# Decay attention and max-of-three experts on one core: the attended tokens of a later batch are split column part by column part

## The chip, the core and the metric

The kernel runs on one core of a Trainium2 chip. A core has TensorE (PE: matmuls, with a weight load, PEld, ahead of each), VectorE (DVE), ScalarE (ACT), GpSimd (POOL) and SyncE (SP), which here issues all transfers. The metric is the device time of one execution in microseconds, as the median of several runs. [...]

## What is computed

```python
# q, k, v: (8, 8, 576, 64); f: (8, 8, 576)
scores = scale * np.matmul(q, k.transpose(0, 1, 3, 2))
cum = np.cumsum(np.log(np.clip(f, 0.0001, 1.0)), axis=-1)
scores = np.where(causal, -1000000000.0, scores + cum[:, :, :, None] - cum[:, :, None, :])
attn = softmax(scores)                       # with 1e-09 added to the sum
x = np.matmul(attn, v)                       # to (4608 tokens, 512)
h = np.maximum(np.maximum(x @ w1, x @ w2), x @ w3)   # three experts, 512 -> 768
out = h @ w_out                              # 768 -> 512
```

## The kernel before

There are eight batches of eight heads. A batch has 576 tokens and, after attention, 512 features, held as four tiles u of 128 features by 576 tokens (one tile for two heads). Attention of a head works in two units of its 576 queries: unit 2 is queries 0 to 255, unit 1 is queries 256 to 575. Each has a first pass of matmuls (scores), a maximum over keys (DVE, then a POOL all-reduce), a second pass that subtracts it, exponentials on ACT, and, for two heads at a time, the matmuls with the values (line 771 in batch 0, line 802 later) into the one PSUM bank t (mp 132 for unit 2 of batch 0). The sums of a pair of heads go through a small transfer to memory and back, and line 908 multiplies u by their inverse. In batch 0 the division is done in four groups: lines 846 (turning the sums), 861 and 862 (DVE), 850 (widening on ACT), 857 (spreading on PE), 868 (the multiplication on DVE).

The experts need each value of x as a rounded part xh and a remainder xl, because the matmuls take rounded operands: `split_x` copies u to xh on ACT (line 913) and subtracts on DVE (line 915), once for each of the four tiles of a batch, over all 576 columns. There is one buffer xh and one xl, so the split of a batch overwrites that of the batch ahead.

`moe` runs the experts in two runs of columns. An even batch takes columns 0 to 255 and then 256 to 575; an odd one 0 to 319 and then 320 to 575. A run has 18 first-product tiles (`gemm1`, line 939): 12 matmuls each, three for each of the four tiles of x, into one of three PSUM banks (mp 130, 131, 132, in rotation). ACT (line 946) or DVE (line 948, the running maximum of the three experts) empties the bank; then ACT and DVE split the maximum (lines 951, 953). After each run come the output products (`gemm2`, line 968, 18 matmuls for 128 tokens), also into the three banks.

Nothing is issued in the order in which it is written. `Plan.add` collects every step with its engine, a cost, the keys that it reads and writes, and a priority. `Plan.emit` then plays all engines forward with these costs and picks, for each engine, among the steps that are ready the one of lowest rank: its priority less a share (BLW) of the length of what hangs on it. Each engine runs its steps in the resulting order. A key stands for a buffer or a part of one; `plan.parts` says which keys are made of smaller ones, and a step waits for the last writer and, where it writes, for all readers of each of its parts. The priorities are head numbers with offsets: LEAD, UP, VO (values), FO (finishing a pair), XO (split), HP and VP (transfers of heads and values), QP and QP1 (transfers and transposes of four heads, lines 535 to 541), LO (the groups of batch 0), WP and WR (weights, lines 512 to 522), HC, SP_, CB, MLAG and lag. MORE adds a delay to what another engine has to deliver, and LIKE is how far PE goes out of rank to put like matmuls together.

Of the kernel before, what the change touches and what calls it, by code (L numbers as in the profile page):

```python
# [48 lines left out]
class Plan:  # L49
# [9 lines left out]

    ROOM = {"PE": (0.93, 0), "ACT": (1.0, -20.0), "DVE": (1.0, 0.0), "POOL": (1.0, 400.0), "SP": (1.0, 0)}  # L60
    LATE = 350.0
    MORE = (0.0, 100.0, 125.0, 0.0, 250.0)
    LIKE, HOLD = 4.0, 0.4

    def __init__(self):
        self.steps, self.wrote, self.read, self.parts = [], {}, {}, {}
# [20 lines left out]
    def emit(self):  # L87
# [8 lines left out]
        for i in reversed(range(n)):  # L96
            s = self.steps[i]
            down[i] = s[1] + s[5] + max((down[u] + 150 for u in users[i]), default=0.0)
        BLW = 0.19
        rank = [s[4] * 1.0 - BLW * down[i] / 12000 for i, s in enumerate(self.steps)]  # L100
        free, wait, live = {}, {}, {}
        for i, s in enumerate(self.steps):
# [69 lines left out]
def act_cost(cols):  # L172
    return 0.833 * cols + 60


def dve_cost(cols):
    return 1.04 * cols + 68
# [3 lines left out]
def kernel(  # L181
# [15 lines left out]
    nc = tc.nc  # L197
# [21 lines left out]
    for i in range(8):  # L219
        for c in ("q", "k"):  # L220
            plan.parts[f"{c}f{i}"] = [f"{c}f{i}/{x}" for x in range(4)]
            plan.parts[f"{c}s{i}"] = [f"{c}s{i}/{x}" for x in range(4)]
    for i in range(4):
        plan.parts[f"vn{i}"] = [f"vn{i}/{x}" for x in range(3)]
    plan.parts["r"] = ["r/0", "r/1"]
    plan.parts["sc"] = ["sc/0", "sc/1"]
# [81 lines left out]
    def U(i):  # L308
        return UT[i] if i < KT else lazy(f"u{i}", [P, S], F32)
# [10 lines left out]
    def xh(kt):  # L320
        return lazy("xh", [P, KT, S])[:, kt, :]

    def xl(kt):
        return lazy("xl", [P, KT, S])[:, kt, :]
# [583 lines left out]
        add("DVE", dve_cost(S), lambda: nc.vector.tensor_tensor(U(i), U(i), R(), op=ALU.mult), [f"u{i}", "r"], [f"u{i}"], prio)  # L908

    def split_x(b, prio):  # L910
        for kt in range(KT):
            i = (b * KT + kt) % NU
            add("ACT", act_cost(S) + 50, lambda i=i, kt=kt: nc.scalar.activation(xh(kt), U(i), AF.Copy),
                [f"u{i}"], [f"xh{kt}"], prio)
            add("DVE", dve_cost(S), lambda i=i, kt=kt: nc.vector.tensor_tensor(
                xl(kt), U(i), xh(kt).bitcast(F32), op=ALU.subtract), [f"u{i}", f"xh{kt}"], [f"xl{kt}"], prio)


    mcount = [0]
# [7 lines left out]
    def gemm1(b, c0, cn, fb, parts, prio):  # L927
        ti = tmc[0] % 2
        tmc[0] += 1
        t, kt_ = TM[ti][:, 0:cn], f"tm{ti}"  # L930
        early = b < NB32 and c0 == 0
        for i in range(3):
            mp, km = next_mp()
            m = mp[:, 0:cn]
            for kt in range(KT):
                def go(kt=kt, i=i, m=m):
                    hh, ll = (xa(kt), xb(kt)) if early else (xh(kt)[:, c0:c0 + cn], xl(kt)[:, c0:c0 + cn])
                    for x, (w, xx) in enumerate(((0, hh), (0, ll), (1, hh))):
                        nc.tensor.matmul(  # L939
                            m, unit_w(i, fb)[:, w, kt, :], xx,  # L940
                            start=kt == 0 and x == 0, stop=kt == KT - 1 and x == 2,
                        )
                add("PE", 3 * mm_cost(cn, P), go,
                    ([f"xa{kt}", f"xb{kt}"] if early else [f"xh{kt}", f"xl{kt}"]) + [f"wh{3 * fb + i}", f"wl{3 * fb + i}"] + ([km] if kt else []), [km], prio)
            if i == 0:
                add("ACT", act_cost(cn), lambda m=m: nc.scalar.activation(t, m, AF.Copy), [km], [kt_], prio)  # L946
            else:
                add("DVE", dve_cost(cn), lambda m=m: nc.vector.tensor_tensor(t, m, t, op=ALU.max),  # L948
                    [km, kt_], [kt_], prio)
        for hh, hl, kh, kl, a, d, w in parts:  # L950
            add("ACT", act_cost(w) + 40, lambda hh=hh, a=a, d=d, w=w: nc.scalar.activation(  # L951
                hh()[:, fb, d:d + w], t[:, a:a + w], AF.Copy), [kt_], [kh + str(fb)], prio)
            add("DVE", dve_cost(w), lambda hh=hh, hl=hl, a=a, d=d, w=w: nc.vector.tensor_tensor(  # L953
                hl()[:, fb, d:d + w], t[:, a:a + w], hh()[:, fb, d:d + w].bitcast(F32), op=ALU.subtract),
                [kt_, kh + str(fb)], [kl + str(fb)], prio)
# [47 lines left out]
                done += 18 * mm_cost(512, P)  # L1003


    LEAD, MLAG, WP, WR = 2.1, -0.1, 0.7, 0.55
    DP = -10.9
    DPW = 4.0
    ROWS = -4.0
    warm_up()  # L1010
    decay()
    QP = -0.3
    UO = 1
    LO = -2.55
    UP, VO, FO, XO = 0.4, 1.8, 0.25, -3.1
    HP, VP = -1.8, 0.6
    SP_ = 1.25
    HC, VO1, XO1, QP1, CB = -0.8, -1.0, -2.3, 0.7, -0.15
    order = (1, 2) if UO else (2, 1)
    for n in range(H):  # L1020
        load_raw(n, n - 9.9)
    for n in range(H):
        turn_head(n, n - 5.6)
        if n % 2 == 0:
            load_v(n // 2, n - LEAD - VP)
    for unit, up in ((2, 0.0), (1, 0.7)):
        for n in range(H):
            p = n * 0.5 - LEAD + up
            subs = (2,) if unit == 2 else ("a", "b") if 0 else ("b", "a")
            for x in subs:  # L1030
                scores(n, x, p)
            for x in subs:
                values(n, x, p + VO1)
            if n % 4 == 3:
                finish_group(n // 4, unit, p + LO)
# [15 lines left out]
    retire(["vn1"], [f"hdh{x}" for x in fbs])  # L1051
    for t in ("hmh", "hml"):
        retire([c + t for c in ("mx", "pf")] + [f"mx{t}a"], [f"{t}{x}" for x in fbs])
    lag = 0.15
    moe(0, lambda x: H + lag + H * x)
    retire([f"rs{g}{u}" for g in range(2) for u in (1, 2)], ["ph1"])
    retire([f"xa{x}" for x in range(KT)], ["pl1"])
# [11 lines left out]
    for n in range(H, BH):  # L1069
# [14 lines left out]
        if n % 2:  # L1084
            finish_pair(pi, p + FO)
        if h == H - 1:
            split_x(b, p + XO)
            moe(b, lambda x, n=n: n + 1 + MLAG + H * x)
    with tc.manual_schedule():
        plan.emit()  # L1090
# [30 lines left out]
```

## Time and profile before

| | |
|---|---|
| runs | 908.95, 909.64, 911.47 us (median 909.64) |
| the profiled execution | 907.59 us, of which 905.5 us is the span of its instructions |
| split on ACT (line 913) | 28 instructions, 0.68 us each, the first at 189.7 us, the last at 824.6 |
| split on DVE (line 915) | 28 instructions, median 0.754 us, longest 1.273 |

A row of the page for an engine gives its busy time, its share of the span and its number of instructions. A row of the waits is: engine, tile and line, what it waited for, then the total in us, how often, and the longest. A group by line gives the shape of what is written and read, the count, then busy time in us and the mean of one in ns, then the idle time of the engine just before. A row of a timeline gives start and duration in us, and in brackets the engine's idle time before it with what ended it; the record of a matmul is longer than the step from one matmul to the next, since matmuls overlap.

### The profile page before, as it was taken

The numbers are of one execution on the slowest core, as the hardware profiler recorded it, in microseconds if no ns is written. First come the engines' busy times: TensorE is split into PE (matmuls) and PEld (weight loads), VectorE is DVE, ScalarE is ACT, GpSimd is POOL, SyncE is SP. The second block draws the span as 40 slices with busy tenths as digits, with TensorE's granted clock in tenths as the row PEclk, the third lists the DMA queues.
The fourth block names the chain that finished last, engine by engine and source line by source line (L and its number), as shares of the span: only waits on it lengthen the run. The fifth ranks groups of instructions, "written<-read, shape, count | busy, mean of one in ns | idle before, by whom it ended". The sixth has DMA issues, their size and how long they took to land.

```text
span 905.5 us, 18417 instructions
## 1 busy us (share of the span) xinstructions
PE 894.0 (99%) x6682; PEld 808.5 (89%) x6682; DVE 643.5 (71%) x1451; ACT 387.5 (43%) x900; POOL 426.8 (47%) x380
## 2 busy tenths in 40 slices
PE   8999999999999999999999999999999999999998
PEld 6899988889989898988989898998989898998998
DVE  6899985577859786786858887786957678672211
ACT  6886644354334443443434443444434443342111
POOL 5444233336455645646554765556555564650000
PEclk9999999999999999999999999999999999999999
DMA  7955155555454455446445554546434455401000
GB/s 205 319 153 177 45 155 128 149 127 161 97 149 123 116 137 147 121 93 181 95 107 143 134 136 117 153 92 175 98 98 130 117 158 118 105 15 37 1 35 24
DMA packets 96868, 110.32 MB, mean 122 GB/s; under 512 B 51861, under 2 KB 64405, under 8 KB 96778
## 3 DMA queue, kind: packets, MB, share of 16 engines
q1 hardware_dynamic: 96778, 109.15, 45.7%
q8 instruction: 53, 0.87, 0.4%
q14 instruction: 37, 0.30, 0.1%
HBM read 49.56 MB, written 9.86 MB: 66 GB/s over the span
## 4 chain that ended last, share of the span: by engine, by line
PE 94%; DVE 2%; ACT 2%; DMA 1%; issue 1%; SPq 0%; ACTq 0%; DVEq 0%
PE mp L939 50%; PE mp L968 17%; PE s L646 13%; PE t L802 9%; PE t L771 2%; PE t L821 1%; DMA w<-in_moe_w_dram 1%; PE mp L771 1%; PE s L662 0%; ACT hl L539 0%; PE t L857 0%; SPq L438 0%; ACT ph_f L734 0%; PE mp L646 0%; DVE va_s L750 0%
## 5 line engine op out<-in xcount | busy, mean ns | idle before, releaser
L939 PE MATMUL mp<-xh_r,w_r 128*128 128x320 f32 (+1 forms) x2160 | 462.2, 298 | 1.4 <-DVE tm L948 1.4
L939 PEld LDWEIGHTS mp<-xh_r,w_r 128*128 128x128 f32 x2160 | 355.8, 188 | 10.9 <-issue 6.0
L939 PE MATMUL mp<-xl_r,w_r 128*128 128x320 f32 (+1 forms) x1080 | 319.5, 296 | 0.0
L758 POOL PARTITION_ALL_REDUCE z<-va_s x96 | 193.1, 2012 | 162.3 <-DVE va_s L750 61.2
L716 POOL PARTITION_ALL_REDUCE gm<-mx x131 | 158.4, 1211 | 194.8 <-DVE mx L703 77.5
L939 PEld LDWEIGHTS mp<-xl_r,w_r 128*128 128x128 f32 x1080 | 203.3, 188 | 0.5
L948 DVE TENSOR_TENSOR tm<-mp,tm 128x256 f32<-128x256 f32 (+1 forms) x192 | 86.3, 449 | 88.6 <-PE mp L939 83.5
L646 PEld LDWEIGHTS s<-qs_r,ks_r 128*128 128x128 f32 (+1 forms) x784 | 116.1, 181 | 19.5 <-issue 14.3
L646 PE MATMUL s<-qs_r,ks_r 128*128 128x320 f32 (+4 forms) x784 | 132.5, 285 | 0.2 <-issue 0.2
L968 PE MATMUL mp<-w_r,hmh_r 128*128 128x512 f32 (+1 forms) x396 | 122.8, 392 | 0.0
L706 DVE TENSOR_TENSOR mx<-mx,s 128x320 f32<-128x320 f32 (+3 forms) x248 | 92.2, 372 | 18.7 <-PE s L646 6.0
L968 PEld LDWEIGHTS mp<-w_r,hmh_r 128*128 128x128 f32 x396 | 70.1, 188 | 13.6 <-issue 1.8
L951 ACT ACTIVATE hmh_r<-tm 128x256 fp32r<-128x256 f32 x96 | 39.9, 416 | 98.9 <-DVE tm L948 98.4
L968 PE MATMUL mp<-w_r,hml_r 128*128 128x512 f32 (+1 forms) x198 | 76.9, 388 | 0.0
L946 ACT ACTIVATE tm<-mp 128x256 f32<-128x256 f32 (+1 forms) x96 | 39.6, 412 | 80.4 <-PE mp L939 76.2
L535 DVE STREAM_TRANSPOSE hl<-hl 128x576 f32<-128x576 f32 x56 | 68.1, 1241 | 0.8 <-DMA hl<-in_k_dram 0.8
L734 ACT ACTIVATE pf<-s 128x512 f32<-128x512 f32 (+4 forms) x107 | 48.8, 505 | 37.5 <-PE s L646 34.5
L953 DVE TENSOR_TENSOR hml_r<-tm,hmh_r 128x256 fp32r<-128x256 f32 x96 | 48.5, 506 | 18.1 <-ACT hmh_r L951 17.5
L719 POOL CAST qs_r<-gm 1x256 fp32r<-1x256 f32 (+1 forms) x112 | 56.8, 508 | 7.1
L675 DVE TENSOR_TENSOR s<-s,mask 128x256 f32<-128x256 f32 x96 | 40.6, 423 | 23.6 <-PE s L646 23.2
L734 ACT ACTIVATE ph_f<-s 128x384 f32<-128x384 f32 x80 | 36.0, 505 | 44.6 <-PE s L646 44.5
L713 ACT ACTIVATE mx<-s 128x320 f32<-128x320 f32 x56 | 24.4, 436 | 51.8 <-DVE s L680 44.1
(213 smaller groups left out, 1261.6 us busy)
## 6 DMA issues: line engine op xcount, KB each, us to landing
qs_r<-hl SPq DMA_DIRECT2D x168, 144.0 KB
ks_r<-hl SPq DMA_DIRECT2D x168, 144.0 KB
w<-in_moe_w_dram SPq DMA_DIRECT2D x18, 512.0 KB
out_dram<-o_r SPq DMA_DIRECT2D x35, 256.0 KB
hl<-in_q_dram SPq DMA_DIRECT2D x14, 576.0 KB
hl<-in_k_dram SPq DMA_DIRECT2D x14, 576.0 KB
r_r<-rdram SPq DMA_DIRECT2D x56, 144.0 KB
vn<-in_v_dram SPq DMA_DIRECT2D x30, 128.0 KB
```

Source lines behind the costliest of these rows:

```text
L535: add("DVE", 1085, lambda e=e, tt=tt, xs=xs: nc.vector.transpose(tt[:, e], xs[:, e]), [key + "0"], [key + "1"], prio)
L646: nc.tensor.matmul(bank[bk][0:l.shape[-1], col:col + w], l, rhs(qa, w), start=start and bk not in begun, stop=stop, skip_group_check=True)
L706: nc.vector.tensor_tensor(mt[:, a:a + w], mt[:, a:a + w], bank[bk][:, col:col + w], op=ALU.max)
L716: add("POOL", 450 + 2.6 * nq, lambda: nc.gpsimd.partition_all_reduce(gm, mt, P, bass.bass_isa.ReduceOp.max), [km, km + "a"], [kg], prio - CB)
L719: add("POOL", 130 + 0.9 * nq, lambda: nc.gpsimd.tensor_copy(QS(s)[96:97, 1, q0:q0 + nq], gm[96:97, :]), [kg], [kx], prio - CB)
L734: add("ACT", act_cost(w), lambda bk=bk, w=w, col=col: nc.scalar.activation(px()[:, col:col + w], bank[bk][:, 0:w], AF.Exp, scale=sc), [kb[ ...
L758: add("POOL", 520 + 5.1 * nq, lambda: nc.gpsimd.partition_all_reduce(Z[:, q0:q0 + nq], blocks_sum()[:, q0:q0 + nq], P, bass.bass_isa.Reduc ...
L802: nc.tensor.matmul(t[D * j:D * j + D, qa:qa + w], vn[:, j, c, 0:D], prs[j][0]()[:, col:col + w], start=x == 0, stop=True, skip_group_check ...
L939: nc.tensor.matmul(m, unit_w(i, fb)[:, w, kt, :], xx, start=kt == 0 and x == 0, stop=kt == KT - 1 and x == 2,)
L948: add("DVE", dve_cost(cn), lambda m=m: nc.vector.tensor_tensor(t, m, t, op=ALU.max), [km, kt_], [kt_], prio)
L953: add("DVE", dve_cost(w), lambda hh=hh, hl=hl, a=a, d=d, w=w: nc.vector.tensor_tensor(hl()[:, fb, d:d + w], t[:, a:a + w], hh()[:, fb, d:d ...
L968: nc.tensor.matmul(mp[:, 0:cn], l[:, fb, cs], unit_o(fb)[:, r, ds], start=fb == 0 and x == 0, stop=fb == FT - 1 and x == 2,)
```

## The change

The split of a later batch is made in parts of columns, with a key for each part of xh and xl (0: columns 0 to 255, 1: 256 to 319, 2: 320 to 575). Ahead of an even batch there are two pieces for each tile, columns 0 to 255 and 256 to 575; ahead of an odd batch three, 0 to 255, 256 to 319 and 320 to 575. A first-product step reads only the keys of the columns of its run, so that a piece of the next batch's split waits only for the run that reads its columns. The first piece has its own priority offset (XO), the others XO + X2. Some twenty of the plan's constants change with it.

```diff
-    MORE = (0.0, 100.0, 125.0, 0.0, 250.0)
-    LIKE, HOLD = 4.0, 0.4
+    MORE = (0.0, 100.0, 125.0, 50.0, 250.0)
+    LIKE, HOLD = 3.5, 0.4
...
-        BLW = 0.19
+        BLW = 0.25
...
+        for t in "hl":
+            plan.parts[f"x{t}{i}"] = [f"x{t}{i}/{x}" for x in range(3)]
...
-        for kt in range(KT):
-            i = (b * KT + kt) % NU
-            add("ACT", act_cost(S) + 50, lambda i=i, kt=kt: nc.scalar.activation(xh(kt), U(i), AF.Copy),
-                [f"u{i}"], [f"xh{kt}"], prio)
-            add("DVE", dve_cost(S), lambda i=i, kt=kt: nc.vector.tensor_tensor(
-                xl(kt), U(i), xh(kt).bitcast(F32), op=ALU.subtract), [f"u{i}", f"xh{kt}"], [f"xl{kt}"], prio)
+        for x, c0, cn in ((0, 0, S2), (1, S2, S1)) if b % 2 == 0 else ((0, 0, S2), (1, S2, 64), (2, S1, S2)):
+            ks = ["0"] if x == 0 else ["1", "2"] if cn == S1 else [str(x)]
+            for kt in range(KT):
+                i = (b * KT + kt) % NU
+                cs, ku = slice(c0, c0 + cn), f"u{i}/{1 + (x == 0)}"
+                kh, kl = ([f"x{t}{kt}/{k}" for k in ks] for t in "hl")
+                add("ACT", act_cost(cn) + 50, lambda i=i, kt=kt, cs=cs: nc.scalar.activation(xh(kt)[:, cs], U(i)[:, cs], AF.Copy),
+                    [ku], kh, prio(x))
+                add("DVE", dve_cost(cn), lambda i=i, kt=kt, cs=cs: nc.vector.tensor_tensor(
+                    xl(kt)[:, cs], U(i)[:, cs], xh(kt)[:, cs].bitcast(F32), op=ALU.subtract), [ku] + kh, kl, prio(x))
...
-                    ([f"xa{kt}", f"xb{kt}"] if early else [f"xh{kt}", f"xl{kt}"]) + [f"wh{3 * fb + i}", f"wl{3 * fb + i}"] + ([km] if kt else []), [km], prio)
+                    ([f"xa{kt}", f"xb{kt}"] if early else [f"x{t}{kt}/{k}" for t in "hl" for k in "012" if c0 <= (0, S2, S1)[int(k)] < c0 + cn]) + [f"wh{3 * fb + i}", f"wl{3 * fb + i}"] + ([km] if kt else []), [km], prio)
...
-    LEAD, MLAG, WP, WR = 2.1, -0.1, 0.7, 0.55
-    DP = -10.9
+    LEAD, MLAG, WP, WR = 2.1, -0.1, 0.4, 0.45
+    DP = -11.15
...
-    QP = -0.3
+    QP = -0.5
...
-    LO = -2.55
-    UP, VO, FO, XO = 0.4, 1.8, 0.25, -3.1
-    HP, VP = -1.8, 0.6
-    SP_ = 1.25
-    HC, VO1, XO1, QP1, CB = -0.8, -1.0, -2.3, 0.7, -0.15
+    LO = -3.35
+    UP, VO, FO, XO = 0.4, 1.4, 0.25, -2.6
+    HP, VP = -2.8, 1.6
+    SP_ = 1.75
+    X2 = -0.5
+    HC, VO1, XO1, QP1, CB = 0.6, -1.0, -2.3, -0.3, 0.35
...
-    for unit, up in ((2, 0.0), (1, 0.7)):
+    for unit, up in ((2, 0.0), (1, 1.0)):
...
-    lag = 0.15
+    lag = 0.3
...
-            split_x(b, p + XO)
+            split_x(b, lambda x: p + XO + (0.0 if x == 0 else X2))
```

Three places show how the order of instructions moves. In the changed file the same statements stand two lines lower up to `finish_pair` (L535 is L537, L908 is L910) and seven lines lower in the experts (L948 is L955); the split is L922.

The first place is DVE at the change from batch 0 to batch 1, where three of the four tiles of x are there. Before:

```order
L948 TENSOR_TENSOR tm_123<-mp_131,tm_123 128x320
L953 TENSOR_TENSOR hml_r<-tm_123,hmh_r 128x256
L953 TENSOR_TENSOR hdl_r<-tm_123,hdh_r 128x64
L908 TENSOR_TENSOR u_89<-u_89,r_r 128x576
L915 TENSOR_TENSOR xl_r<-u_r,xh_r 128x576
L675 TENSOR_TENSOR s_128<-s_128,mask 128x2x128
L680 TENSOR_TENSOR s_126<-s_126,mask 128x64
L701 COPY mx_83<-s_128 128x128
```

Now:

```order
L955 TENSOR_TENSOR tm_123<-mp_131,tm_123 128x320
L960 TENSOR_TENSOR hml_r<-tm_123,hmh_r 128x256
L960 TENSOR_TENSOR hdl_r<-tm_123,hdh_r 128x64
L910 TENSOR_TENSOR u_89<-u_89,r_r 128x576
L922 TENSOR_TENSOR xl_r<-u_89,xh_r 128x256
L922 TENSOR_TENSOR xl_r<-u_r,xh_r 128x256
L922 TENSOR_TENSOR xl_r<-u_r,xh_r 128x64
L922 TENSOR_TENSOR xl_r<-u_88,xh_r 128x64
L922 TENSOR_TENSOR xl_r<-u_88,xh_r 128x256
L677 TENSOR_TENSOR s_128<-s_128,mask 128x2x128
L682 TENSOR_TENSOR s_126<-s_126,mask 128x64
L703 COPY mx_83<-s_128 128x128
```

One subtraction of a whole tile ahead of the masks has become five of parts; the first parts of the two other tiles were made some thirty to sixty instructions earlier.

The second place is PE in the second run (256 columns) of batch 1: w6, w7 and w9 are the weights of tiles that follow one another in the program, mp1 and mp2 two of the three banks. Before:

```order
L939 MATMUL mp1_131<-xl_r_1200,w6_r_695 128x256
L939 MATMUL mp1_131<-xh_r_978,w6_r_695 128x256
L939 MATMUL mp2_132<-xh_r_978,w7_r_699 128x256
L939 MATMUL mp2_132<-xl_r_1200,w7_r_699 128x256
L939 MATMUL mp2_132<-xh_r_978,w7_r_699 128x256 x2
```

Now:

```order
L946 MATMUL mp1_131<-xl_r_1171,w6_r_670 128x256
L946 MATMUL mp1_131<-xh_r_982,w6_r_670 128x256
L946 MATMUL mp1_131<-xh_r_982,w9_r_837 128x256
L946 MATMUL mp1_131<-xl_r_1171,w9_r_837 128x256
L946 MATMUL mp1_131<-xh_r_982,w9_r_837 128x256 x2
```

Before, the tile of w7 lies between two tiles of the bank mp1; now the tile of w9 follows that of w6 on the same bank, and w7 comes after it.

The third place is ACT at the second group of batch 0, where u_88 and u_89 from t are the copies that empty the bank t, and the L539 row is the rounding of four heads' transposed keys or queries. Before:

```order
L512 ACTIVATE w_107<-w_107 128x512
L539 ACTIVATE hl<-hl 128x1152
L783 ACTIVATE u_88<-t 64x160
L785 ACTIVATE ph_79<-t 1x160
L850 ACTIVATE rx<-hdl 128x256
```

Now:

```order
L785 ACTIVATE u_89<-t 64x160
L787 ACTIVATE ph_79<-t 1x160
L736 ACTIVATE pf_80<-s_126 128x480
L514 ACTIVATE w_109<-w_109 128x512
L736 ACTIVATE pf_80<-s_127 128x224
L541 ACTIVATE hl<-hl 128x1152
L852 ACTIVATE rx<-hdl 128x256
```

Before, the rounding stands in front of a copy from t; now it stands behind those copies and in front of the widening.

More of the change, by code (lines that the diff above doesn't have):

```diff
@@ L1011 @@
     decay()
-    QP = -0.3
+    QP = -0.5
     UO = 1
-    LO = -2.55
-    UP, VO, FO, XO = 0.4, 1.8, 0.25, -3.1
-    HP, VP = -1.8, 0.6
-    SP_ = 1.25
-    HC, VO1, XO1, QP1, CB = -0.8, -1.0, -2.3, 0.7, -0.15
+    LO = -3.35
[4 more added lines that the diff above has]
+    HC, VO1, XO1, QP1, CB = 0.6, -1.0, -2.3, -0.3, 0.35
     order = (1, 2) if UO else (2, 1)
     for n in range(H):
-        load_raw(n, n - 9.9)
+        load_raw(n, n - 10.1)
     for n in range(H):
```

## The prediction

> **What bounds the kernel now.** I read the page first, its span, its engines and the slices.
>
> ```profile
> span 905.5 us, 18417 instructions
> ...
> PE 894.0 (99%) x6682; PEld 808.5 (89%) x6682; DVE 643.5 (71%) x1451; ACT 387.5 (43%) x900; POOL 426.8 (47%) x380
> ...
> PEclk9999999999999999999999999999999999999999
> ```
>
> TensorE is busy for 894.0 of 905.5 us, and the granted clock never drops. No other engine is near its limit. So the change can win only part of 905.5 - 894.0 = 11.5 us, unless it changes the matmuls themselves. The next view cuts the span into seven stretches, to see where the 11.5 us lie.
>
> ```profile
> core 0: us, PE busy (x) PEld busy (x) DVE busy (x) ACT busy (x) POOL busy (x), PEclk, DMA share, GB/s
> 0.00:26.00 26.00, 22.23 (x264) 17.21 (x264) 17.43 (x39) 17.70 (x38) 13.98 (x32) 1.00 0.76 205
> 26.00:60.00 34.00, 31.28 (x243) 28.61 (x242) 32.71 (x66) 29.50 (x69) 15.23 (x15) 1.00 0.84 262
> 60.00:130.00 70.00, 70.00 (x620) 66.84 (x620) 67.25 (x139) 42.92 (x98) 25.92 (x25) 1.00 0.46 129
> 130.00:390.00 260.00, 259.72 (x1967) 233.06 (x1961) 187.94 (x425) 108.77 (x255) 129.16 (x114) 1.00 0.51 131
> 390.00:400.00 10.00, 8.65 (x65) 7.27 (x64) 7.33 (x16) 2.94 (x9) 5.38 (x3) 1.00 0.63 140
> 400.00:820.00 420.00, 419.85 (x2985) 377.57 (x2983) 312.23 (x727) 170.20 (x397) 237.10 (x192) 1.00 0.46 119
> 820.00:905.50 85.50, 82.32 (x559) 77.94 (x555) 18.61 (x44) 15.45 (x39) 0.00 (x0) 1.00 0.06 22
> ```
>
> Span minus PE busy gives the idle time of each stretch: 26.00 - 22.23 = 3.8 us at the start, 2.7 us from 26 to 60, then nothing to 130, 0.3, 1.35, 0.15, and 3.2 us at the end. The list of what TensorE waited for names the pieces:
>
> ```profile
> PE mp L471 <- DVE qs L479: 1.5, 1, 1.5
> PE mp L939 <- DVE tm L948: 1.4, 1, 1.4
> PE t L771 <- ACT ph L785: 1.0, 1, 1.0
> PE mp L857 <- DVE u L868: 0.9, 1, 0.9
> PE mp L771 <- DVE u L868: 0.7, 1, 0.7
> ```
>
> The last stretch is the tail behind the last attention pass. Here the chain of work shows the bare rhythm of the experts, which prices everything below:
>
> ```profile
> 824.01 31.68 PE mp L939 x216
> 855.69 12.55 PE mp L968 x54
> 868.25 25.55 PE mp L939 x216
> ```
>
> A first-product matmul of 320 columns takes 31.68/216 = 0.147 us, one of 256 columns 25.55/216 = 0.118, an output matmul of 512 columns 12.55/54 = 0.232.
>
> **The split itself.** The order of the changed kernel holds the same matmuls in the same shapes, so no TensorE work goes or comes. The split grows from 28 pairs of instructions to 72: four odd batches have 12 pieces in place of 4, three even ones 8. The prices are the means of the groups kept apart by shape, VectorE's first, then ScalarE's.
>
> ```profile
> L915 DVE TENSOR_TENSOR xl_r<-u,xh_r 128x576 fp32r<-128x576 f32 x22 | 17.1, 797 | 8.7 <-ACT xh_r L913 8.6
> L953 DVE TENSOR_TENSOR hml_r<-tm,hmh_r 128x256 fp32r<-128x256 f32 x96 | 48.5, 506 | 18.1 <-ACT hmh_r L951 17.5
> L953 DVE TENSOR_TENSOR hdl_r<-tm,hdh_r 128x64 fp32r<-128x64 f32 x48 | 18.7, 390 | 1.6 <-ACT hdh_r L951 1.6
> ```
> ```profile
> L951 ACT ACTIVATE hmh_r<-tm 128x256 fp32r<-128x256 f32 x96 | 39.9, 416 | 98.9 <-DVE tm L948 98.4
> L913 ACT ACTIVATE xh_r<-u 128x576 fp32r<-128x576 f32 x22 | 14.8, 681 | 3.6 <-PE mp L939 3.5
> L951 ACT ACTIVATE hdh_r<-tm 128x64 fp32r<-128x64 f32 x48 | 11.9, 247 | 22.5 <-DVE tm L948 22.5
> ```
>
> On VectorE one quarter of an odd batch goes from 0.80 to 0.51 + 0.39 + 0.51 = 1.40 us, of an even one to 0.51 plus some 0.57 for 320 columns (an estimate between the 256 and the 576 row) = 1.08. That is 16 x 0.60 + 12 x 0.28 = 13 us more on VectorE. ScalarE gets 16 x 0.40 + 12 x 0.20 = 9 us more. Both are far from full (643.5 and 387.5 us), so I cost this at nothing. What hides it: at each of the seven changes of batch, both orders put 36 output matmuls between the last first-product of one batch and the first of the next, 36 x 0.232 = 8.4 us, and the whole split of a batch needs some 3 to 6 us. If that cover were gone, the last piece of each change would stand open, about 0.25 + 0.39 us and two handovers, 7 x 0.8 = 6 us. The same count of 36 says what the early halves do not bring: the next batch starts no sooner after the last one. Their gain is nothing too.
>
> **An added wait.** A piece of the split waits for the last matmul that read the old columns. VectorE runs in order; behind such a piece stand the maxima (L948 before, L955 now) that empty the matmul banks, and TensorE waits for those. Before shows what a late maximum costs:
>
> ```profile
> 393.02 2.26 POOL L758 PARTITION_ALL_REDUCE z<-va_s  x1 [0.39 <-DVE va_s L750]
> 393.18 1.40 DVE L953 TENSOR_TENSOR hdl_r<-tm,hdh_r 128x64 fp32r<-128x64 f32 x1
> 393.38 0.31 PE L939 MATMUL mp<-xh_r,w_r 128*128 128x320 f32 x1
> 394.51 1.07 DVE L948 TENSOR_TENSOR tm<-mp,tm 128x320 f32<-128x320 f32 x2
> 395.04 0.41 PE L939 MATMUL mp<-xh_r,w_r 128*128 128x320 f32 x1 [1.35 <-DVE tm L948]
> ```
> ```profile
> L953 DVE TENSOR_TENSOR hdl_r<-tm,hdh_r x48: 154/218/1404, 144.4 to 856.5; 128x64 fp32r<-128x64 f32 x48
> ```
>
> The second view gives minimum, median and maximum of the same instruction: 0.218 us is usual. Here it took 1.40 beside a GpSimd all-reduce, the maximum behind it began 1.1 us after TensorE's last matmul, and 395.04 - 393.38 - 0.147 = 1.5 us were lost. [...]
>
> In the new order the steady part is also tighter at places. I walked through both orders with the three prices above and measured, for each bank, the matmul time from a tile's last matmul to the next tile's first. Before, the smallest is 1.05 us. Now five are below 0.9: 0.0, 0.2, 0.2, 0.4 and 0.9 us, the first being the second place shown above (w6, then w9, both on mp 131). The bank needs the matmul's record of 0.31 us, an eviction and two handovers of about 0.05 (394.51 plus half of 1.07 to 395.04 bounds one). The evictions:
>
> ```profile
> L946 ACT ACTIVATE tm<-mp 128x256 f32<-128x256 f32 x48 | 18.5, 386 | 41.4 <-PE mp L939 41.2
> ```
>
> 0.31 + 0.39 + 0.10 = 0.8 us, less the 0.12 that belong to the matmul itself: about 0.7 us lost where nothing lies between, then 0.5, 0.5, 0.3 and 0. I add **2.0 us** (bounds 0, if real timing pulls them apart, and 4, if VectorE is late there as well). Against that, the waits of before from 130 to 820 go with their places: 0.3 + 1.35 + 0.15 idle and some 0.16 for each of four that a record's overhang hides (0.31 - 0.147), **-2.4 us**. Holds like that at 393 will fall elsewhere; I give them back at **+0.5** (0 to 2.4).
>
> **The start.** Up to 26 us the two orders of TensorE are the same, so its 3.8 us stay. From 26 to 60 us two chains cost 2.7 us:
>
> ```profile
> 41.30 0.68 PE L857 MATMUL mp<-hdl,rx 128*128 128x128 f32 x4 [0.87 <-DVE u L868]
> 42.70 0.86 PE L771 MATMUL mp<-hmh,vl 128*65 128x128 f32 x4 [0.73 <-DVE u L868]
> ...
> 56.23 0.47 PE L771 MATMUL t<-pf,hdh 128*65 128x64 f32 x3 [1.04 <-ACT ph L785]
> ```
> ```profile
> 54.38 1.17 ACT L539 ACTIVATE hl<-hl 128x1152 fp32r<-128x1152 f32 x1
> 55.57 0.29 ACT L783 ACTIVATE u<-t 64x160 f32<-64x160 f32 x1
> ```
>
> At 42.70 the values of a head waited for bank mp 132 behind the second spreading; in the new order the values behind it use bank t, so that wait goes: 0.73 + 0.16 = **-0.9 us**. At 56.23 TensorE waited for ScalarE to empty t, and ScalarE had the 1.17 us of L539 in front (third place above). Now both copies stand ahead of it: **-1.2 us**. What is late next: L541 now stands in front of the widening (L852) that the second group's spreading waits for. Between the turning (L848) and that spreading the new order has about 1.9 us of matmuls; the chain is turning, two small VectorE steps in a queue 96% full (32.71 of 34.00), 1.17 and 0.42 on ScalarE, together 2.2 to 3.3 us. I take **+0.8** (0.3 to 1.4). The constants also fetch weights earlier and heads later on SP's queue, past the row transfers. By the same walk through the orders, a head's buffer is refilled during 7.8 us of matmuls at the tightest place before and 7.9 now, so I cost this at nothing; were a refill late, each would cost what it is late by, and the table shows no such wait at 130 to 820 us.
>
> **The sum.** Start -0.9 - 1.2 + 0.8 = -1.3; steady part +2.0 - 2.4 + 0.5 = +0.1; switches between kinds of matmul, which the order moves about (passes of 320 columns followed by an expert matmul fall from 102 to 96), 0, bounds -1 and +1; the tail is unchanged. Together **-1.2 us**. The profiled execution took 907.59 us, 905.5 of it the span; the median of the three shown is 909.64, 2.0 above it, so I carry the difference, not the sum: 907.59 becomes 906.4, and the median **908.4 us**.
>
> **Rivals.** *All of it is recovered.* The start's 2.7 us and its hidden 0.5, the steady part's 2.4, and nothing new: -5.6, so 904.0 us. For it: nearly the whole program is reordered and no new matmul appears. Against it: VectorE stays at 96% in the stretch where the start waits, and the order has places without cover.
>
> *The change does not reach the path.* The splits move, 36 output matmuls still separate the batches, the waits of the start change names and keep their size: 0, so 909.6.
>
> *VectorE becomes late at the changes of batch (slower).* Place: the pieces of the split in front of a maximum, five in a row at the first place above. With whole tiles a bank comes round after two others, 24 x 0.147 = 3.5 us, of which the eviction takes 0.31 + 0.48 + 0.05; so it decides when VectorE's queue is late by more than 2.7 us. Five pieces are 0.51 x 3 + 0.39 x 2 = 2.3 us, a hold of 1.2 us more passes the point. Then each of seven changes loses about 0.9 us: -1.2 + 6.3 = +5.1, so 914.7. [...] Against the rival: of 48 short subtractions the median is 0.218 and the mean 0.390, so few are held, and one such hold of before reached TensorE.
>
> **How the numbers follow.** The forecast gets 0.45, the change that does not reach the path 0.15, full recovery 0.23, slow VectorE 0.17. A measurement here tells 0.3%, 2.7 us, from no change: below 906.9 is faster, above 912.4 slower. The first two cases lie within it: 0.60; faster 0.23, slower 0.17. With all bounds the forecast runs from -1.8 - 2.4 - 1 = -5.2 to -0.7 + 4.0 + 1 = +4.3, that is from 904.4 to 913.9; the range reaches down to full recovery, 904.0, and up over part of the slower case, 914.0, and leaves out less than 0.2.
>
> **What would show it.** Right: the matmul list has 6682 entries, idle time from 26 to 60 us falls to some 1.7 us, TensorE's wait list shows the spreading after ScalarE's widening and two to four waits of 0.4 to 0.9 us for a bank from ScalarE or VectorE, and the tail keeps 3.2 us. Wrong in size: no idle beyond the start (full recovery), or a wait of a microsecond at each change of batch with the split's subtraction in front (slow VectorE). It would be wrong in kind if matmuls of the same form took longer, or if a head's refill showed up in the waits.

## The result, and the profile after

| | before | after |
|---|---|---|
| median | 908.92 us (6 runs, 908.21 to 911.47) | 914.99 us (6 runs, 912.66 to 916.82) |
| ratio | | 1.0062, 95% interval 1.0047 to 1.0077 |
| profiled execution, its span | 907.59, 905.5 us | 915.55, 913.8 us |
| mean granted clock | 1.000 in that run | 0.996 in that run; 1.000, 0.996, 0.998, 0.996, 0.996 in the others |

The changed kernel is 0.6% slower. 908.4 us was forecast, with a range up to 914.0, so the time lies above the range. From the page of the changed kernel, the same lines as before:

```profile
span 913.8 us, 18534 instructions
...
PE 898.9 (98%) x6682; PEld 810.4 (89%) x6682; DVE 646.1 (71%) x1495; ACT 392.7 (43%) x944; POOL 421.9 (46%) x380
...
PEclk9999999999999999999999999999999999999999
```

The matmuls are the same 6682. Idle time grew from 11.5 to 913.8 - 898.9 = 14.9 us, and TensorE was 4.9 us longer "busy" with the same matmuls. The forty slices hide why (each digit is the mean of 23 us, and 9 is 90% or more); the seven stretches, with the columns of the prediction's table (PEclk third from the end), show it:

```profile
0.00:26.00 26.00, 22.15 (x251) 17.44 (x253) 17.57 (x39) 17.14 (x36) 14.19 (x32) 0.93 0.73 207
26.00:60.00 34.00, 32.50 (x257) 29.44 (x255) 32.20 (x67) 29.53 (x68) 14.38 (x15) 1.00 0.80 252
60.00:130.00 70.00, 65.70 (x566) 63.71 (x570) 62.72 (x132) 41.08 (x95) 22.14 (x24) 0.98 0.46 116
130.00:390.00 260.00, 258.43 (x1961) 228.65 (x1952) 186.09 (x432) 107.97 (x262) 127.91 (x113) 1.00 0.51 133
390.00:400.00 10.00, 9.87 (x69) 9.61 (x68) 9.88 (x20) 5.92 (x14) 3.97 (x5) 1.00 0.44 104
400.00:820.00 420.00, 419.64 (x2990) 377.95 (x2989) 316.38 (x757) 173.27 (x424) 239.26 (x194) 1.00 0.47 120
820.00:913.80 93.80, 90.61 (x608) 83.63 (x606) 21.24 (x55) 17.82 (x47) 0.00 (x0) 1.00 0.07 24
```

Idle time by stretch is 3.85, 1.5, **4.3**, 1.6, 0.1, 0.4 and 3.2 us, against 3.8, 2.7, 0, 0.3, 1.35, 0.15 and 3.2 before. The stretch from 60 to 130 us, which had none, now has the most, and its clock is below 1, as that of the first 26 us is. Finer windows of the changed kernel find the two places where the clock was halved:

```profile
10.00:20.00 10.00, 9.66 (x126) 8.37 (x126) 4.53 (x12) 6.84 (x18) 2.02 (x3) 0.83 0.81 233
...
75.00:80.00 5.00, 4.38 (x34) 4.15 (x35) 4.62 (x9) 2.56 (x5) 0.00 (x0) 1.00 1.00 195
80.00:85.00 5.00, 2.00 (x19) 1.70 (x17) 2.32 (x5) 3.38 (x8) 1.06 (x1) 1.00 1.03 247
85.00:90.00 5.00, 5.00 (x33) 5.00 (x33) 4.29 (x10) 2.68 (x6) 2.39 (x2) 0.66 0.17 68
```

10 x (1 - 0.83) = 1.7 us of full clock are lost in the one and 5 x (1 - 0.66) = 1.7 in the other. By the trace's clock record each is one halving, to 0.50, that lasts 3.41 us: 11.19 to 14.61 and 86.29 to 89.70 us. At 1.7 of 913.8 us, 0.0019 each, a mean clock of 0.998 over the whole run stands for one of them, 0.996 for two; where they lie is known for the profiled run alone. So the 8.3 us between the two spans are 3.4 us more idle time, 3.4 us of halved clock, and a rest of 1.5 us, presumably inside the records of matmuls (0.16 us at each wait for a bank, as the prediction worked out). The list of waits names the idle time (left out are 1.5 us twice at the start, as before):

```profile
PE s L648 <- DMA ks_r<-hl: 3.0, 1, 3.0
PE mp L946 <- ACT tm L953: 1.7, 4, 0.5
...
PE s L648 <- ACT pf L736: 0.9, 2, 0.6
PE t L773 <- ACT pf L736: 0.7, 1, 0.7
PE mp L859 <- ACT rx L852: 0.6, 1, 0.6
```

The first line is new and the largest: the first scores of head 8, the first head of batch 1, waited for a transfer of K. TensorE's timeline there:

```profile
80.31 1.40 PE L773 MATMUL t<-pf,vl 128*65 128x64 f32 x10
84.70 0.45 PE L648 MATMUL s<-qs_r,ks_r 128*128 128x256 f32 x2 [3.00 <-DMA ks_r<-hl]
...
86.54 2.80 PE L648 MATMUL s<-xl 128*128 128x160 f32 x10
```

The ten matmuls from 86.54 on take 2.80 us (1.50 in the run with the filled wait, at a clock of 1.00); that is the halved clock, right behind the wait. Now SP's queue, which issues the transfers (start, time to issue, line, what is moved, how many), in the changed kernel:

```profile
71.94 0.60 SPq L510 DMA_DIRECT2D w<-in_moe_w_out_dram  x1
73.06 2.85 SPq L568 DMA_DIRECT2D qs_r<-hl  x4
75.96 0.72 SPq L510 DMA_DIRECT2D w<-in_moe_w_out_dram  x1
76.79 1.48 SPq L568 DMA_DIRECT2D ks_r<-hl  x2
78.31 1.11 SPq L510 DMA_DIRECT2D w<-in_moe_w_out_dram  x2
```

and in the kernel before:

```profile
65.32 0.58 SPq L566 DMA_DIRECT2D ks_r<-hl  x1
66.36 0.40 SPq L508 DMA_DIRECT2D w<-in_moe_w_dram  x1
...
68.17 1.33 SPq L566 DMA_DIRECT2D ks_r<-hl  x2
...
70.06 2.06 SPq L508 DMA_DIRECT2D w<-in_moe_w_out_dram  x4
```

Before, all transfers of K for heads 8 and 9 went out ahead of the first load of w_out (512 KB each). Now two loads of w_out stand ahead of the last two transfers of K and two right behind them, and the DMA engines were full from 75 to 85 us (shares of 1.00 and 1.03). The last two transfers of K could hardly have been issued sooner where they stand, since they read the subtraction of VectorE that ended at 75.27 + 1.35 = 76.62 us:

```profile
75.27 1.35 DVE L543 SCALAR_TENSOR_TENSOR hl<-hl 128x1152 fp32r<-128x1152 f32 x1
```

By the diff none of this is the split: WP and WR time the weights' loads and the steps behind them, QP1 the four heads' loads and subtractions in batch 1.

### The profile page after: what moved, and what is told of

Read it like the earlier page. It is cut to its first block, busy times and chain, and to the rows that moved or that the text cites. A ratio compares the mean times of both kernels' runs of the same rounds, so it can differ in the third digit from the quotient of the medians.

```text
span 913.8 us, 18534 instructions
## 1 busy us (share of the span) xinstructions
PE 898.9 (98%) x6682; PEld 810.4 (89%) x6682; DVE 646.1 (71%) x1495; ACT 392.7 (43%) x944; POOL 421.9 (46%) x380
## 4 chain that ended last, share of the span: by engine, by line
PE 94%; DMA 2%; DVE 2%; ACT 1%; issue 1%; SPq 0%; ACTq 0%; DVEq 0%
PE mp L946 50%; PE mp L975 17%; PE s L648 13%; PE t L804 9%; PE t L773 2%; DMA ks_r<-hl 1%; PE t L823 1%; PE mp L773 1%; PE mp L473 1%; DMA vn<-in_v_dram 0%; DMA r_r<-rdram 0%; PE mp L648 0%; PE s L664 0%; PE t L473 0%; ACT tm L953 0%
## 5 line engine op out<-in xcount | busy, mean ns | idle before, releaser
L760 POOL PARTITION_ALL_REDUCE z<-va_s x96 | 190.7, 1987 | 185.1 <-DVE va_s L752 56.1
L955 DVE TENSOR_TENSOR tm<-mp,tm 128x256 f32<-128x256 f32 (+1 forms) x192 | 86.5, 451 | 92.0 <-PE mp L946 74.7
L648 PEld LDWEIGHTS s<-qs_r,ks_r 128*128 128x128 f32 (+1 forms) x784 | 116.5, 181 | 21.1 <-issue 11.7
L648 PE MATMUL s<-qs_r,ks_r 128*128 128x320 f32 (+4 forms) x784 | 130.8, 284 | 3.0 <-DMA ks_r<-hl 3.0
L537 DVE STREAM_TRANSPOSE hl<-hl 128x576 f32<-128x576 f32 x56 | 69.2, 1242 | 0.4 <-DMA hl<-in_q_dram 0.4
L721 POOL CAST qs_r<-gm 1x256 fp32r<-1x256 f32 (+1 forms) x112 | 54.1, 486 | 6.9
```

The costliest lines, as they stand in the source:

```text
L537: add("DVE", 1085, lambda e=e, tt=tt, xs=xs: nc.vector.transpose(tt[:, e], xs[:, e]), [key + "0"], [key + "1"], prio)
L648: nc.tensor.matmul(bank[bk][0:l.shape[-1], col:col + w], l, rhs(qa, w), start=start and bk not in begun, stop=stop, skip_group_check=True)
L721: add("POOL", 130 + 0.9 * nq, lambda: nc.gpsimd.tensor_copy(QS(s)[96:97, 1, q0:q0 + nq], gm[96:97, :]), [kg], [kx], prio - CB)
L760: add("POOL", 520 + 5.1 * nq, lambda: nc.gpsimd.partition_all_reduce(Z[:, q0:q0 + nq], blocks_sum()[:, q0:q0 + nq], P, bass.bass_isa.Reduc ...
```

## The experiments

Theory A: the time comes from the start of batch 1, the wait for K and the halved clock behind it. Its two forms: A1, the transfer is late because of the loads of w_out around it; A2, because of VectorE's late subtraction. Theory B, the main rival: the time comes from the split at the changes of batch. All runs in one table, each with the kernel before run beside it; the last column counts runs whose mean granted clock was 0.999 or more.

| run | median us (runs) | before beside it | ratio, 95% interval | full clock |
|---|---|---|---|---|
| split alone | 913.01 (6) | 908.45 | 1.0045, 1.0031 to 1.0060 | 1 of 6 |
| numbers alone | 916.98 (6) | 908.45 | 1.0092, 1.0076 to 1.0108 | 2 of 6 |
| one load behind | 910.29 (11) | 908.45 | 1.0020, 1.0009 to 1.0030 | 10 of 11 |
| weights later | 909.33 (12) | 908.45 | 1.0008, 1.0000 to 1.0017 | 11 of 12 |
| filled wait | 911.85 (12) | 909.12 | 1.0025, 1.0013 to 1.0038 | 10 of 12 |
| third load ahead | 914.71 (4) | 909.12 | 1.0061, 1.0038 to 1.0085 | 1 of 4 |
| numbers, weights later | 913.29 (8) | 909.12 | 1.0043, 1.0029 to 1.0058 | 7 of 8 |
| start restored | 913.57 (6) | 909.12 | 1.0044, 1.0027 to 1.0061 | 3 of 6 |
| bank lag | 910.71 (12) | 909.32 | 1.0019, 1.0010 to 1.0028 | 9 of 12 |
| bank lag, old rank | 930.82 (4) | 909.32 | 1.0240, 1.0219 to 1.0260 | 0 of 4 |
| before, start filled | 908.47 (12) | 908.77 | 0.9987, 0.9975 to 1.0000 | 8 of 12 |
| weights later, start filled | 909.60 (12) | 908.77 | 1.0002, 0.9992 to 1.0012 | 12 of 12 |

**Split alone**: the new `split_x`, parts and keys, every number as before (X2 = 0).

> The split into halves with all numbers of the plan as before. Theory A (the time comes from the numbers that place batch 1's first transfers): batch 1 starts as before, so no wait of TensorE for K between 60 and 130 us, and 907 to 911 us. Theory B (the time comes from the split, whose extra pairs on ScalarE and VectorE are late at the changes of batch): 912.5 to 916 us, with TensorE idle or slow at 187, 287, 391 and 496 us.

913.01 us: theory A's number missed, and B's hit, though not at B's places. Up to 130 us it runs like before, without idle time from 60 to 130. Its largest loss is at 625 us; its timeline and windows there:

```profile
625.95 0.45 PE L648 MATMUL s<-qs_r,ks_r 128*128 128x256 f32 x2 [1.06 <-POOL qs_r L721]
626.29 0.42 PE L946 MATMUL mp<-xh_r,w_r 128*128 128x320 f32 x1
627.18 0.41 PE L946 MATMUL mp<-xl_r,w_r 128*128 128x320 f32 x1 [0.48 <-DVE xl_r L922]
```
```profile
626.00:632.00 6.00, 5.52 (x27) 5.25 (x27) 4.64 (x11) 2.12 (x8) 4.22 (x4) 0.72 0.18 38
```

1.5 us of waits and 6 x 0.28 = 1.7 us of clock make some 3.2 of the 4.5 us. Only the shorter wait is for the split's xl; the longer one is for a row that GpSimd writes into the queries' buffer. With the old numbers the order that has the split costs 4.5 us; but this place is not in the changed kernel, whose list of waits names neither xh nor xl.

**Numbers alone**: all numbers of the diff, `split_x` in one piece.

> The numbers of the change with the split in one piece, as before. Theory A: the first heads of batch 1 stand in the same order as in the changed kernel, so TensorE waits about 3.0 us for K at 82 us, a cut of its clock follows in most runs, and it takes 912.5 to 916 us. Theory B: 907 to 911 us. If both halves of the change cost, each comes out about 3 us above before.

916.98 us, above the range of both theories, with "ks_r<-hl: 2.2" at the top of TensorE's waits. Theory A holds for the start: that of the changed kernel, a wait for K included, comes without the split. It does not hold for the rest of the time: the list also has 1.5 us without a named cause, at 721 us, and 1.1 us for xl. The profiled run had this wait and no halving (clock 1.000); 4 of 6 runs had a clock of 0.998 or 0.996. Both halves cost alone, and together they cost less than their sum (4.5 + 8.5 against 6.1 us), so they are not two separate prices.

**One load behind**: the changed kernel with one row of SP's order moved and no other engine's. `held` is the second load of w_out, `ahead` the last transfers of K for heads 8 and 9.

```diff
         self.span = max(free.values())
+        for k, i in enumerate(self.held):
+            old, begin[i] = begin[i], max(begin[j] for j in self.ahead) + 0.001 * (k + 1)
...
+            if step in (19,):
+                plan.held.append(len(plan.steps) - 1)
...
+        if n in (8, 9):
+            plan.ahead.append(len(plan.steps) - 1)
```

> The changed kernel with one thing moved: the second load of w_out (512 KB) stands behind the last two transfers of K for heads 8 and 9 instead of ahead of them; no other engine's order changes. If the wait at 82 us is for bytes queued ahead (A1): at the 195 to 250 GB/s of that stretch the load takes 2.1 to 2.7 us, so the wait falls from 3.0 us to 0.3 to 0.9 us, the cut of the clock behind it (1.7 us) goes in most runs, and the time is 910.5 to 913 us. If it is for VectorE's late subtraction, which ends at 76.6 us (A2): the transfers are issued at the same time and the wait stays near 3.0 us, 914 to 916 us.

910.29 us, 4.7 less than the changed kernel and just below A1's range. SP's queue, then TensorE's wait for K between 60 and 95 us (the statements stand lower in this file: L655 is L648, L573 is L568, L513 is L510):

```profile
71.60 2.74 SPq L573 DMA_DIRECT2D qs_r<-hl  x4
75.20 1.23 SPq L573 DMA_DIRECT2D ks_r<-hl  x2
76.47 1.54 SPq L513 DMA_DIRECT2D w<-in_moe_w_out_dram  x3
```
```profile
PE s L655 <- DMA ks_r<-hl: 0.2, 1, 0.2
```

The wait fell from 3.0 to 0.2 us, and 10 of 11 runs had the full clock against 1 of 6. The transfers were still issued right behind the subtraction, which ended at 75.18 us here (73.83 + 1.35); that this is 1.4 us earlier than in the changed kernel is no gain, since the changed kernel's profiled run had lost 1.7 us at 11 us. So A2 falls as the cause of the wait: the subtraction only sets when the transfers can go out. One load's place in a queue is worth about 4 of the 6.1 us: 4.7 between the two medians, 6.07 - 1.84 = 4.2 when each is compared with the kernel before run beside it.

**Weights later**: WP 0.4 to 0.7 and WR 0.45 to 0.55, their old values, in the changed kernel.

> The changed kernel with the two numbers that time the weights' loads back at their old values (0.7 and 0.55): all six transfers of K for heads 8 and 9 stand ahead of the first load of w_out. Theory A1: no wait for K over 0.5 us between 60 and 130 us, 908 to 911.5 us. A2: the subtraction is still late, a wait of 1 to 3 us stays, 912 to 915 us. Theory B: 913 to 916 us whatever the wait does.

909.33 us: no wait for K there, and 0.9 us above before, at the edge of its interval. This run does not tell A1 from A2, though: the subtraction ended at 68.47 us here (67.13 + 1.34) and the last transfers of K went out at 71.68 us, so both causes are gone at once.

**Filled wait**: is the halved clock a consequence of the wait?

```diff
         def pass_a(banks):
+            if n == H and unit == 2:
+                z = ident.rearrange("p (o x) -> p o x", o=1).broadcast_to((P, 4, P))
+                for _ in range(12):
+                    nc.tensor.matmul(SP2.rearrange("p (o x) -> p o x", o=4), ident, z, start=True, stop=True)
```

> The changed kernel with 12 matmuls of the identity (512 columns, bf16, into the bank that the next scores overwrite) just ahead of head 8's first scores, where TensorE stood 3.0 us; three such matmuls took 0.82 us at 9.57 us, so 12 take 2.6 to 3.3 us. They add work and compute nothing. If the idle time brings the cut of the clock (C1): the wait for K falls under 0.6 us, the K lands no earlier, the cut at 86 us is gone in most runs, and the time is 912 to 914 us. If the cut comes whatever TensorE does there (C2): the cut stays and it is 914.5 to 916 us.

Its timeline, then the window behind it (L777 is L773, L661 the filling):

```profile
79.36 1.40 PE L777 MATMUL t<-pf,vl 128*65 128x64 f32 x10
80.60 2.75 PE L661 MATMUL s<-ident 128*128 128x512 bf16 x12
83.42 0.45 PE L648 MATMUL s<-qs_r,ks_r 128*128 128x256 f32 x2
```
```profile
85.00:90.00 5.00, 5.00 (x47) 5.00 (x45) 4.79 (x12) 3.75 (x9) 3.21 (x3) 1.00 0.18 45
```

From the values to the scores TensorE took 83.42 - 79.36 = 4.06 us, against 84.70 - 80.31 = 4.39 in the changed kernel, so next to nothing of the wait was won. The time fell to 911.85 us nevertheless, just below C1's range, the clock behind the place is whole (1.00 where the changed kernel has 0.66), and 10 of 12 runs had the full clock, beside 1 of 4 in the next kernel, which ran on the same chip with the wait left idle. So C1, for this place: with TensorE's idle time filled, the cut behind it is gone in most runs. Idle time does not bring it every time: the profiled run of the next kernel has the wait of 3.0 us and a clock of 1.000. Open is why most runs of the filled kernel have no cut at the start either, where nothing was filled and the changed kernel's profiled run has one.

**Third load ahead**: one more load of w_out moved in front of the last two transfers of K, again nothing else.

> The changed kernel with the third load of w_out (512 KB) put ahead of the last two transfers of K for heads 8 and 9, so that three loads stand ahead of them instead of two; no other engine's order changes. A1 (bytes queued ahead): the wait at 82 us grows by what the removed load took off it (2.8 us in the run with one load behind), to 5.2 to 6.2 us, and the time is 917 to 919 us. A2 (VectorE's late subtraction): still 3.0 us, 914 to 916 us.

SP's queue and TensorE's timeline of this run:

```profile
74.61 1.07 SPq L513 DMA_DIRECT2D w<-in_moe_w_out_dram  x2
75.78 1.24 SPq L573 DMA_DIRECT2D ks_r<-hl  x2
77.06 0.62 SPq L513 DMA_DIRECT2D w<-in_moe_w_out_dram  x1
```
```profile
82.75 0.42 PE L655 MATMUL s<-qs_r,ks_r 128*128 128x256 f32 x2 [3.00 <-DMA w<-in_moe_w_out_dram]
```

914.71 us and a wait of 3.0 us again: A1, as I had put it, missed, and both of A2's numbers were met. A2 had fallen in the run with one load behind, so what falls here is A1's price: bytes queued ahead don't count one by one (taking one load away took 2.8 us off the wait, putting one more ahead added nothing). (The row names a load of w_out, which the scores do not read; the last packet of K ended at 82.21 us.) The traces' DMA packets suggest why. K's and Q's packets have 2304 bytes here, those of w_out 4096; packets and bytes are counted from the beginning of K's first packet to that of its last:

```
                      the 128 packets of K   w_out packets begun     all bytes in
                      begin to end, us       meanwhile, mean us      that time
two loads ahead       80.15 to 84.17         130, 0.31               214 GB/s   (the changed kernel)
three loads ahead     79.50 to 82.21          95, 0.27               266 GB/s
one load ahead        76.91 to 79.77          67, 0.34               215 GB/s
none ahead            73.03 to 74.59           2                     208 GB/s   (weights later)
w_out by itself       84.0 to 85.5           134, 0.17               367 GB/s   (the changed kernel)
heads by themselves   71.5 to 73.0             -                     207 GB/s   (the changed kernel)
```

Beside packets of the heads a packet of w_out takes 0.27 to 0.34 us instead of 0.17. With a third load ahead K begins later after its issue (79.50 - 75.78 = 3.7 us against 80.15 - 76.79 = 3.4), but its packets then need 2.7 us instead of 4.0, with 95 packets of w_out begun meanwhile instead of 130. So it lands 0.95 us sooner after its issue; that the wait is 3.0 us in both owes something to chance, since the changed kernel's profiled run had lost 1.7 us at 11 us and TensorE came to these scores 1.95 us later there, while K was issued only 1.0 us later. As I read the table, what delays K is all loads that run ahead of it or beside it; only the run with none gives K its 1.6 us.

**Numbers, weights later**: the run with the weights later, with the split in one piece.

> The numbers of the change with the split in one piece and the weights' loads at their old times: the same as the run with the weights later, less the split. Its start is that run's, so no wait for K over 0.5 us. If the split is worth something once the start is mended (D1): 1 to 3 us above that run's 909.33, that is 910.3 to 912.5 us. If it is worth nothing (D2): 908.5 to 910.3 us. If it costs (D3, which the run with the split alone suggests, 4.5 us above before): below 908.5 us.

913.29 us: with a mended start the halves are worth 3 to 4 us against the whole split (3.2 by the ratios, 1.0043 against 1.0008; 4.0 by the medians), more than D1 said. Part of it is seen: here a first product waits for the whole split's subtraction, as none does in the run with the halves. From its timeline:

```profile
627.52 0.42 PE L939 MATMUL mp<-xl_r,w_r 128*128 128x320 f32 x1 [1.10 <-DVE xl_r L915]
```

**Start restored**: QP1, HP, HC, VP, WP and WR at their old values in the changed kernel.

> The changed kernel with all six numbers that place batch 1's first quad, heads, values, constants and the weights at their old values; the first loads of the quad and the six transfers of K go out in the old order again. Theory A: no wait for K, the gain of 1.0 us between 26 and 60 us is kept or lost with it, 907.5 to 910 us. If the rest of the change costs by itself (B): 910.5 to 913 us.

913.57 us, above A's range and above B's: no wait for K, but the planner laid everything behind the start out anew, with waits of 1.3 us (exponentials), 1.0 (xl), 0.9 (xh) and 0.9 us (u) and halved clock at 8.9 and 60.1 us (mean clock 0.996). Putting numbers back does not put an order back.

**Bank lag**: the run with the weights later, MORE 0.0 to 50.0 for TensorE. It tests what the tight banks are worth, the prediction's +2.0.

> The run with the weights later, with 50 ns more of lag for TensorE in the planner's rule, so that a bank of products counts as free that much later and its next matmuls are placed behind other work: the places where a bank is taken again within 0.2 us fall from four (0.0, 0.0, 0.18, 0.18 us) to none. If those places are what is left of the loss once the start is mended (E1): they cost 0.5 to 0.7 us each there, so 1.8 to 2.5 us less than that run's 909.33, 906.8 to 907.6 us, and below before. If they are not (E2): within 0.8 us of 909.33.

910.71 us, outside both ranges and 1.4 us above the run with the weights later (1.0 by the ratios). E1 falls: the waits "ACT tm" are gone from the list, and nothing was won, since others came. From its waits:

```profile
PE mp L946 <- ACT o_r L982: 1.4, 1, 1.4
PE s L648 <- ACT pf L736: 1.3, 1, 1.3
...
PE mp L946 <- DVE xl_r L922: 1.0, 1, 1.0
```

**Bank lag, old rank**: the same with BLW 0.19 and QP -0.3.

> The same with two more numbers at their old values (the weight of the rest of the chain, 0.19, and the time of the quads' loads, -0.3): the same start, no bank taken again within 0.6 us either. E1: 906.5 to 907.8 us. E2: 908.5 to 910.5 us.

930.82 us, far off both. Its waits and one of its windows:

```profile
PE s L648 <- POOL qs_r L721: 6.1, 2, 5.6
PE s L648 <- DMA ks_r<-cdram: 4.2, 2, 3.1
```
```profile
425.00:430.00 5.00, 3.45 (x17) 3.11 (x19) 3.35 (x8) 2.17 (x6) 2.73 (x3) 0.50 0.38 91
```

Heads that come late again, now in the steady part, at 425 and 642 us, and the clock halved for 10.2 us from inside the first of these waits on (0.84 from 420 to 425 us, 0.50, then 0.63 from 430 to 435), and for 6.8 us at the second (a mean clock of 0.991 over 927.9 us is 16.7 us at half for both). So neither run tells what the tight banks alone are worth.

**Start filled**: six such matmuls where TensorE stands 1.5 us at 7.4 us, once in the kernel before and once in the run with the weights later.

> The kernel before with 6 matmuls of the identity (512 columns, bf16) where TensorE stands 1.5 us at 7.4 us, into a bank that the warm-up used. They compute nothing. Of 59 runs of the kernel before, 29 had a granted clock of 0.999 or more (median 908.1 us) and 30 less (909.8 us); in three profiled runs a cut of 3.41 us began at 8.9 to 11.2 us. If idle time brings that cut (C1): at least 8 in 10 runs at 0.999 or more, median 907.7 to 908.3 us. If not (C2): half the runs are cut as before, 908.5 to 909.5 us.

> The changed kernel with the weights later and the same 6 matmuls at 7.4 us. C1 as above; that run's clock was already 0.999 or more in 11 of 12, so the time stays at 909.0 to 909.6 us. If the fill itself costs (the bank, the order behind it): over 909.8 us.

In the kernel before:

```profile
7.67 1.47 PE L472 MATMUL s<-ident 128*128 128x512 bf16 x6
9.07 0.72 PE L475 MATMUL mp<-hdl,w 96*64 96x96 f32 x12
```

8 of 12 runs at full clock and none under 0.998, against 11 of 23 and 8 of 23 (0.997 or less) for before beside it: between C1's number and C2's, so that idle time brings the cut at the start too is not shown. 908.47 us, 0.9987 of before, with 1.0 at the end of the interval, is the lowest ratio of the study, but not shown to be a gain. The mended change with the fill takes 909.60 us and can't be told from before (0.9992 to 1.0012).

## Why the prediction was wrong

*TensorE bounds it*: right, 98% now. But "the granted clock never drops" was read from one execution. Of the 82 runs of before whose clock is known, 40 had 0.999 or more (35 at 1.000, median 908.13 us), 25 had 0.998 (909.56), 11 had 0.996 (910.94), and the other six had 0.997 or 0.994: none to three cuts of 1.7 us. The profiled execution was one without a cut. I carried the 2.0 us between it and the median along as a constant; part of it is the price of such cuts, and of the changed kernel's six runs five had one or two.

*The split at nothing*: the count was right (44 more on each engine). No wait of the changed kernel names xh or xl, so it was covered there. As a property of the split it was wrong: with the old numbers its order costs 4.5 us, and with the new ones and a mended start the halves save 3 to 4.

*The 1.5 us at 395*: right, idle time from 390 to 400 us fell from 1.35 to 0.13.

*Tight banks, +2.0*: right. Three of the four waits "ACT tm" (0.53, 0.36 and 0.35 us at 287, 340 and 496 us) stand where 0.0, 0.2 and 0.2 us of matmuls lie between two uses of a bank, and 0.7, 0.5 and 0.5 less the 0.16 that a record hides were foretold; the fourth, 0.47 us at 75 us, lies ahead of the steady part. The run with the bank lag took such waits away and won nothing.

*Start from 26 to 60, -1.3*: idle time fell from 2.7 to 1.5 us, where 1.7 was forecast; the new wait for the widening is 0.6 where 0.8 was taken. That the total fits is luck in part: the 0.87 us at line 857, which I kept, went, and two waits for exponentials (line 736: 0.66 and 0.33 us), which I had not foreseen, came.

**The step that failed** is "the constants also fetch weights earlier and heads later on SP's queue ... so I cost this at nothing". It priced a refill by the matmul time between two uses of a head's buffer, 7.8 and 7.9 us, and looked for waits at 130 to 820 us. The first filling of the buffers, for heads 8 and 9, has no earlier use and lies ahead of 130 us; there the room is what SP's queue leaves. The rows to be read stood in the new order of SP: two loads of 512 KB ahead of K's last transfers, none before. It also priced a late refill at what it is late by, where the cut of the clock came on top. That step cost 4.2 to 4.7 us by the run with one load behind, which is about 3.0 of wait and 1.7 for the cut that follows it, and 5.2 to 5.7 by the run with the weights later, in which other things moved too. Without it the change takes 909.3 to 910.3 us, inside the forecast's range, but 0.9 to 1.8 us above before where 1.2 below was forecast. The sentence that a refill in the waits would make it wrong in kind did apply.

*The rivals*: slow VectorE gave 914.7 us and the right sign, by a mechanism that the changed kernel does not show; the variants have one or two waits of 0.5 to 1.6 us for xl, not one at each change of batch.

*Open*: what makes up the 0.9 to 1.8 us that remain with a mended start. The tight banks and the waits at 70 to 80 us are candidates; no run separates them.

## What to carry to other kernels

When a change moves transfers in one queue, print that queue's order at the first filling of every buffer too, and count all bytes that run ahead of a needed transfer or beside it, not only how often the buffer is reused. A wait on the engine that bounds this kernel cost more than its length: 3.0 us of wait, and 1.7 us of clock, halved for 3.41 us behind it; so read the granted clock of every run, not of one. And where a planner sets the order, a constant has no price of its own: test a single moved row before believing one.

## What the runs showed of the hardware

- Halvings of TensorE's clock (to 0.50) were 3.41 us long in the changed kernel, 1.7 us lost for each, and two and three times as long, 6.8 and 10.2 us, in the worst run, the one with the bank lag and the old rank. One began 1.6 us behind the end of a wait of 3.0 us in the changed kernel (84.70 and 86.29 us), one behind waits of 1.06 and 0.48 us in the run with the split alone (clock 0.72 from 626 to 632 us). The one of 10.2 us began some 3.6 us into a wait of 5.56 us that ended at 425.38 us, if the 0.84 from 420 to 425 us is its first 1.6 us. Not every execution with the same order had one: one of six of the changed kernel ran at 1.000, and so did the profiled run with the third load ahead, which had a wait of 3.0 us.
- In the changed kernel's trace the clock's record starts, at full, at 4.37 us, and the two halvings begin 6.83 and 81.92 us later, 2 and 24 times 3.413 us. In the 3.41 us just ahead of them TensorE was idle for 1.49 us (7.78 to 11.19) and 1.83 us (82.87 to 86.29). Idle time in such a step does not decide it alone: in the kernel before, whose record starts at 5.03 us, the eleventh step (39.16 to 42.58 us) had 1.47 us of it and no halving followed. What else decides is not shown.
- Transfers within SBUF (K) and loads from memory (w_out) that ran together took longer: a load's packet of 4096 bytes 0.31 us in the changed kernel (0.27 and 0.34 in the runs with three loads and one ahead) instead of 0.17, K's 128 packets 4.0 us (2.7 and 2.9) instead of 1.6 in the run with the weights later, and the mix moved 214 to 266 GB/s where the loads by themselves had 367.
